# Batch 0's attention in its own order, and its global values from the common gather

## The chip, the cores and the metric

The kernel runs on one core of one Trainium2 chip. The metric is device time in microseconds (us) of one execution; several executions are timed and their median is given. The profile is one further execution, taken by the hardware profiler. Engines are named as in the profile: PE is TensorE, DVE is VectorE, ACT is ScalarE, POOL is GpSimd and SP is SyncE; PEq, DVEq and so on are their sequencers.

## The reference

Two layers are computed one after the other. The first is attention with a local window and eight global tokens, over 8 batches, 8 heads, 576 tokens and a head size of 64:

```
scores = q @ k.T / sqrt(64)
mask   = |i - j| <= 32, or i is global, or j is global
attn   = softmax(scores where mask, else -1e9)
x      = attn @ v                      # (4608 tokens, 512)
```

The second takes x through two matrix products with a periodic activation between them:

```
h   = x @ w_in                         # 512 -> 2048
g   = h + sin(alpha*h)**2 / (alpha + 1e-9)
out = g @ w_out                        # 2048 -> 512, f32
```

## The kernel before, in words

The kernel goes through the batches in order. `phase_a(b, b - 1)` computes the attention of batch b and fills TensorE's spare time with the second matrix product (`gemm2`, handed out in small steps by `fill`) of the batch before; `gemm1(b)` then computes the first matrix product and the activation of batch b in 16 groups of 128 hidden columns. All instructions are issued in an order written out by hand: each engine takes its own in program order, so an instruction that waits holds up all behind it on its engine. DMA queues are two: POOL issues the loads that convert from f32 to bf16, SP all others, each in program order as well.

**Attention (L840 to L1000).** Heads are taken in four pairs. `scores(hp, g)` (L862) computes one half of a pair's scores into a PSUM tile of two banks, ACT takes the exponential (L881), and DVE multiplies by the 0/1 mask (L882). `denominators` (L938) multiplies the exponentials by ones; ACT takes the logarithm (L830) and DVE sums the global columns (L814). `inverse` (L943) is an exponential of the negative logarithm on ACT (L837). `numerators` (L946) multiplies the exponentials by the values (L910), for batches 0 and 1 also by the global values `VGT` (L926), and DVE normalises into `xT` (L953). PSUM has the tiles `zn`, `zd` and `ring` (or, after `ring` is released, `zr`) of two banks and `zo[0]`, `zo[1]` of one. In batch 0 the first scores go to `ring`, the second scores of pairs 0 and 1 to `zn`, and those of pairs 2 and 3 to `ring`, since numerators use `zn`. The numerators of pair 0 are computed between the two scores of pair 3.

**What batch 0 does beside its scores.** `beside(at)` in `phase_a` (L1285) is called after each pair. For batch 0 it turns the keys and queries of pairs 2 and 3 with TensorE transposes from `lie[0]`, a stretch of `H2`, into `zo` (L681), and copies them to `KX` and `QX` (L688, L695). After pair 1 `first_values` (L759) builds the global values of batch 0: `g0["v"]`, an indirect DMA of batch 0's rows alone (L628), is spread and masked on DVE (L761), a product with the 0/1 matrix `pick` (L620) puts each row into its place, and DVE copies the bank to `VGT[0]` (L623). After pairs 2 and 3, half of the heads each time, DVE copies the odd value rows (`odd_rows`, L416) and the edge tiles (`edge_tiles`, L423) within the value buffer `VF[0]`, which `load_v0` fills with twelve DMAs from POOL (L396).

**The common gather.** SP gathers the rows of the eight global tokens for all batches: keys, queries, values (`gather_heads`, L538; `gather`, L544), each as eight DMAs of which one brings 64 rows of 256 bytes. A DMA of `gather_heads` writes to 64 partitions, one of `gather` to eight. POOL casts them (L772 to `gkq`, L775 to `VGb`) when batch 0's `gemm1` is under way; `turn_kq` (L777) transposes keys and queries on TensorE into `zo[1]`, DVE copies them out (L789), and POOL places batch 1's (L378, L381).

**`gemm1(0)` (L1086 to L1159).** Group nt takes one of `zn`, `zr`, `zd` in turn (L1104), ACT computes Sin (L1148), ACT or DVE squares it (L1151, L1153), DVE adds and writes `H2` (L1154). Lists name the groups that carry other work: `TURNED` transposes a pair of batch 1 into `zo`, `PLACED` copies it out, `GLOBALS` has `turn_kq`; after the last group of the batch stands the picking of batch 1's global values (L1128, with the copy on ACT).

**Others that the change touches.** `warm(z, n)` (L603) issues n products of 512 columns whose result is not used. `find_columns` (L1164) is seven small DVE instructions (L1168 to L1180) that run after the last pair of batch 3's attention.

## Time and profile before

| what | us |
|---|---|
| median of three runs | 356.49 (354.37 to 357.08) |
| the profiled execution's own time | 354.67 |
| its span, first to last instruction | 352.9 |
| batch 0's first scores begin | 11.55 |
| batch 0's first Sin (group 0 of `gemm1(0)`) | 37.38 |
| batch 0's last Sin (group 15) | 58.83 |
| batch 1's first scores begin | 60.38 |

Three views are used. The page gives the busy time of each engine over the span. The chain of waits goes back from the last instruction, at each step to what released it, and is listed in order of time: start, length, and the engine, tile and line. The timeline lists instructions in order of time, neighbours of one line merged (x2 means two): start, length, engine, line, operation, out<-in, shapes, and in brackets how long the engine had been idle and what ended that. L numbers are lines of the kernel before.

### The profile page before, as it was taken

The page shows a single profiled execution, that of the slowest core. Times are in us where ns is not written, and L with a number is a line of the kernel's source. Part 1 is how long each engine was busy: PE and PEld are TensorE (multiplying, and loading weights), DVE is VectorE, ACT ScalarE, POOL GpSimd, SP SyncE. Part 2 cuts the span into 40 slices and gives each one's busy share as a digit, 9 for nine tenths or more (in the row PEclk, how much of TensorE's full clock was granted, in tenths as well). Part 3 has the DMA queues.
Part 4 walks back from the last instruction along what each step waited for, and adds up shares of the span by engine and source line. Part 5 has one row for each costly group of instructions (what it writes and reads, how often), then busy time and mean ns, then how long its engine had stood idle before and what let it go on. Part 6 is the DMA issues. An engine that isn't in the chain of part 4 may idle for free.

```text
span 352.9 us, 11594 instructions
## 1 busy us (share of the span) xinstructions
PE 311.5 (88%) x4783; PEld 203.8 (58%) x4843; DVE 278.4 (79%) x544; ACT 282.1 (80%) x408; POOL 56.4 (16%) x89
## 2 busy tenths in 40 slices
PE   0656888889899999979999999899999999999993
PEld 0544665456655676557655675577556755665543
DVE  5977597967998788888888887978797788788940
ACT  9744789878888888978898889989898888888711
POOL 7963001230004000300003000400000000002600
PEclk9999999999999999999999999999999999999998
DMA  7999997799484948499628991792824111010232
GB/s 103 109 167 208 202 233 158 133 172 207 69 159 86 195 91 167 97 194 145 118 63 166 202 125 48 162 180 39 186 53 106 30 32 63 5 31 2 75 91 66
DMA packets 80413, 41.80 MB, mean 118 GB/s; under 512 B 65522, under 2 KB 74082, under 8 KB 79970
## 3 DMA queue, kind: packets, MB, share of 16 engines
q0 software_dynamic: 38992, 18.51, 41.3%
q1 hardware_dynamic: 41362, 22.48, 28.4%
q8 instruction: 39, 0.64, 0.7%
q14 instruction: 20, 0.16, 0.2%
HBM read 41.87 MB, written 20.77 MB: 178 GB/s over the span
## 4 chain that ended last, share of the span: by engine, by line
PE 68%; DVE 14%; ACT 7%; issue 7%; DMA 1%; POOL 1%; DVEq 0%; POOLq 0%; ACTq 0%
PE zo L1203 27%; PE zn L1104 13%; PE zr L1104 9%; PE zd L1104 9%; PE ring L872 3%; DVE H L1154 3%; ACT sb L1148 2%; PE zn L910 2%; PE zd L910 2%; DMA g0k<-in_k_dram,grow 1%; ACT E L881 1%; DVE s L1153 1%; DVE QX L363 1%; DVE E L882 1%; DVE xT L953 1%
## 5 line engine op out<-in xcount | busy, mean ns | idle before, releaser
L1203 PE MATMUL zo<-w_out,H 128*128 128x512 bf16 (+1 forms) x516 | 134.0, 376 | 6.0 <-issue 5.2
L1104 PEld LDWEIGHTS <-w_in 128*128 128x128 bf16 x1024 | 100.1, 98 | 49.9 <-issue 14.8
L1203 PEld LDWEIGHTS <-H 128*128 128x128 bf16 x592 | 53.6, 98 | 46.1 <-POOL H L1193 0.2
L1104 PE MATMUL zn<-xT,w_in 128*128 128x288 bf16 (+1 forms) x384 | 57.8, 290 | 7.2 <-DVE GN L814 3.9
L881 ACT ACTIVATE E<-ring 128x720 bf16<-128x720 f32 x48 | 37.4, 780 | 15.3 <-PE ring L872 14.5
L1104 PE MATMUL zr<-xT,w_in 128*128 128x288 bf16 x320 | 48.5, 290 | 0.2 <-DVE H L1154 0.2
L1148 ACT ACTIVATE sb<-zn,alphaT 128x576 bf16<-128x576 f32 (+1 forms) x48 | 35.6, 742 | 14.7 <-PE zn L1104 14.3
L1154 DVE SCALAR_TENSOR_TENSOR H<-s,recipT,zn 128x576 bf16<-128x576 bf16 (+1 forms) x48 | 39.5, 822 | 9.9 <-ACT s L1151 5.9
L1104 PE MATMUL zd<-xT,w_in 128*128 128x288 bf16 x320 | 46.3, 288 | 1.0 <-DVE H L1154 0.9
L1153 DVE TENSOR_TENSOR s<-sb 128x576 bf16<-128x576 bf16 (+1 forms) x70 | 32.7, 467 | 11.4 <-ACT sb L1148 11.1
L1151 ACT ACTIVATE s<-sb 128x576 bf16<-128x576 bf16 (+1 forms) x58 | 40.0, 689 | 1.8
L882 DVE TENSOR_TENSOR E<-E,MASKT 128x720 bf16<-128x720 bf16 x64 | 33.4, 529 | 9.1 <-ACT E L881 7.4
L1154 DVE SCALAR_TENSOR_TENSOR H<-s,recipT,zd 128x576 bf16<-128x576 bf16 (+1 forms) x40 | 32.9, 822 | 7.8 <-ACT s L1151 5.3
L1154 DVE SCALAR_TENSOR_TENSOR H<-s,recipT,zr 128x576 bf16<-128x576 bf16 (+1 forms) x40 | 32.9, 822 | 5.7 <-ACT s L1151 4.1
L1148 ACT ACTIVATE sb<-zd,alphaT 128x576 bf16<-128x576 f32 (+1 forms) x40 | 29.5, 738 | 5.8 <-PE zd L1104 5.8
L1148 ACT ACTIVATE sb<-zr,alphaT 128x576 bf16<-128x576 f32 (+1 forms) x40 | 29.6, 739 | 4.9 <-PE zr L1104 4.9
L1210 ACT COPY osb<-zo 128x512 f32<-128x512 f32 (+1 forms) x36 | 20.9, 582 | 11.2 <-PE zo L1203 7.5
L872 PEld LDWEIGHTS <-KX 64*64 64x64 bf16 x896 | 16.1, 112 | 20.6 <-issue 20.4
L837 ACT ACTIVATE R<-L,shift 128x576 f32<-128x576 f32 x32 | 24.9, 782 | 0.4
L348 POOL COPY seen<-xT 1x1 bf16<-1x1 bf16 x4 | 1.9, 480 | 136.4 <-DVE GN L814 136.4
L1193 POOL COPY H<-H 128x11 bf16 (+1 forms) x16 | 7.2, 452 | 98.7 <-DVE H L1154 97.9
L953 DVE TENSOR_TENSOR xT<-zn,R 128x576 bf16<-128x576 f32 x24 | 18.1, 754 | 3.0 <-PE zn L926 2.0
(179 smaller groups left out, 361.1 us busy)
## 6 DMA issues: line engine op xcount, KB each, us to landing
VF<-vd SPq DMA_DIRECT2D x24, 168.0 KB
kd<-in_k_dram POOLq DMA_DIRECT2D x6, 576.0 KB, 6.1
qd<-in_q_dram POOLq DMA_DIRECT2D x6, 576.0 KB, 11.6
vd<-in_v_dram POOLq DMA_DIRECT2D x6, 576.0 KB, 15.2
w_in<-in_moe_w_in_dram POOLq DMA_DIRECT2D x2, 1024.0 KB
w_out<-in_moe_w_out_dram POOLq DMA_DIRECT2D x2, 1024.0 KB, 22.2
out_dram<-osb SPq DMA_DIRECT2D x7, 256.0 KB
out_dram<-osb SPq DMA_DIRECT2D x8, 224.0 KB
```

The lines of the kernel that those rows point to most:

```text
L837: nc.scalar.activation(out=R[:], in_=L[:], func=AF.Exp, scale=-1.0, bias=shift[:, 0:1])
L872: nc.tensor.matmul(out=z[half * D : (half + 1) * D, t, 0 : G3 * WCOL].rearrange("p (m x c) -> p m x c", x=2, c=60)[:, m % G3, :, c0:c1], l ...
L881: nc.scalar.activation(out=Eg, in_=z[:, :, 0 : G3 * WCOL], func=AF.Exp, scale=scale)
L882: nc.vector.tensor_tensor(out=Eg, in0=Eg, in1=MASKT[:, None, G3 * g : G3 * (g + 1), :].rearrange("p o m c -> p o (m c)").to_broadcast([P, ...
L953: nc.vector.tensor_tensor(out=xT[:, hp, 0:S].rearrange("p (k m c) -> p k m c", k=4, c=KT), in0=tokens(nd(hp, 0)), in1=Rs[hp][:], op=ALU.mult,)
L1104: nc.tensor.matmul(out=h_part, lhsT=w_in[:, c, nt * P : (nt + 1) * P], rhs=xT[:, c, lo:hi], start=(c == 0), stop=(c == CT - 1), skip_group ...
L1148: nc.scalar.activation(out=sb[:, 0:W], in_=h, func=AF.Sin, scale=alphaT[:, nt : nt + 1])
L1151: nc.scalar.activation(out=s2[:, 0:W], in_=sb[:, 0:W], func=AF.Square)
L1153: nc.vector.tensor_tensor(out=s2[:, 0:W], in0=sb[:, 0:W], in1=sb[:, 0:W], op=ALU.mult)
L1154: nc.vector.scalar_tensor_tensor(out=H2[:, nt, r0 : r0 + W], in0=s2[:, 0:W], scalar=recipT[:, nt : nt + 1], in1=h, op0=ALU.mult, op1=ALU.add,)
L1203: nc.tensor.matmul(out=ops[:, cols], lhsT=H2[:, nt, blk * P : (blk + 1) * P], rhs=w_out[:, nt, cols], start=(nt == 0), stop=(nt == NT - 1) ...
L1210: nc.scalar.copy(out=osb[:, cols], in_=ops[:, cols])
```

## The change

1. Batch 0's attention has an order of its own (`first_batch`). All scores come first, alternating between `ring` and `zn`; denominators of pair hp - 1 follow the scores of pair hp. Then `ring` is released, and inverses and numerators of pairs 0 and 1 follow, the denominators of pair 3, the numerators of pair 2, those of pair 3. Numerators use `zr` (pairs 0 and 2), `zn` (pair 1) and `zd` (pair 3). Between these steps stand eleven products of `warm`; the one of before is gone.
2. Beside the scores: pairs 2 and 3 are turned after pairs 0 and 2 (keys copied on DVE, queries on ACT); after pair 1 stands only the reciprocal of alpha; after pair 3 the global values are picked and the odd rows and edge tiles of all heads are copied at once.
3. The indirect gather of batch 0's values, its spreading on DVE and the tiles for it are gone. SP's common gather of the values moves ahead of those of keys and queries, and POOL's cast of them stands between the loads of the two halves of `w_in`. `pick[:, 0]` is now masked to batch 0's rows as `pick[:, 1]` was to batch 1's.
4. In `gemm1(0)`: batch 1's global values are picked at group 1 (copy on DVE), where the cast of keys and queries stands as well; `turn_kq` moves from group 12 to 3, with batch 1's placing of globals, the loads of batch 1's values and batch 2's keys and queries behind it; the turning of batch 1's pairs moves by two groups.
5. `find_columns` moves from batch 3's attention to group 8 of `gemm1(2)`.

```diff
--- before.py
+++ after.py
@@ -581,18 +581,16 @@
         out=rowf[0 : NG * B, 4:5], in0=rowf[0 : NG * B, 0:1], scalar=float(S), in1=rowf[0 : NG * B, 3:4], op0=ALU.mult, op1=ALU.add
     )
     nc.vector.tensor_copy(out=grow[:], in_=rowf[0 : NG * B, 4:5])
-    mine = setup.tile([NG * B, B], DT.bfloat16, name="mine")
-    own = rowf[0 : NG * B]
-    nc.vector.tensor_scalar(out=mine[:], in0=jrow[0 : NG * B], scalar1=own[:, 0:1], scalar2=None, op0=ALU.is_equal)
-    one = setup.tile([NG * B, 1], DT.float32, name="one")
-    nc.vector.tensor_scalar(out=one[:], in0=own[:, 0:1], scalar1=1.0, scalar2=None, op0=ALU.is_equal)
-    nc.vector.tensor_scalar(
-        out=pick[:, 0], in0=place8[0 : NG * B], scalar1=own[:, 2:3], scalar2=None, op0=ALU.is_equal
-    )
-    nc.vector.tensor_scalar(
-        out=pick[:, 1], in0=place8[0 : NG * B], scalar1=own[:, 2:3], scalar2=one[:, 0:1], op0=ALU.is_equal,
-        op1=ALU.mult,
-    )
+    of_batch = setup.tile([NG * B, 2], DT.float32, name="of_batch")
+    for b in range(2):
+        nc.vector.tensor_scalar(
+            out=of_batch[:, b : b + 1], in0=rowf[0 : NG * B, 0:1], scalar1=float(b), scalar2=None, op0=ALU.is_equal
+        )
+    for b in range(2):
+        nc.vector.tensor_scalar(
+            out=pick[:, b], in0=place8[0 : NG * B], scalar1=rowf[0 : NG * B, 2:3], scalar2=of_batch[:, b : b + 1],
+            op0=ALU.is_equal, op1=ALU.mult,
+        )
     nc.vector.memset(KX[0][:, :, :, NK:D], 0.0)
     nc.vector.memset(VE[0][:], 0.0)
     nc.vector.memset(shift[:], -SHIFT * LN2)
@@ -622,7 +620,7 @@
     def place_picked(b, z, copy):
         copy(out=VGT[b][:].rearrange("p h d -> p (h d)"), in_=z[:])
 
-    g0 = {name: setup.tile([NG * B, D], DT.bfloat16, name="g0" + name) for name in ("k", "q", "v")}
+    g0 = {name: setup.tile([NG * B, D], DT.bfloat16, name="g0" + name) for name in ("k", "q")}
 
     def rows_of(name, src):
         nc.gpsimd.indirect_dma_start(
@@ -637,9 +635,11 @@
     for half in range(2):
         nc.gpsimd.iota(qpos[half * D : half * D + D], pattern=[[KT, NT6], [1, 2], [2, 24]], base=half * HALF,
                        channel_multiplier=0, allow_small_or_imprecise_dtypes=True)
-    rows_of("v", v)
+    gather(v, gv)
     load_v0()
-    load_w_in((0, 1))
+    load_w_in((0,))
+    nc.gpsimd.tensor_copy(out=VGb[:], in_=gv.rearrange("p h d -> p (h d)"))
+    load_w_in((1,))
     for hps in (early, late):
         for w in (1, 0):
             load_lying(1, w, hps)
@@ -648,7 +648,6 @@
     load_w_out((1,))
     gather_heads(k, gk)
     gather_heads(q, gq)
-    gather(v, gv)
 
 
     band = setup.tile([P, 2, 2, WCOL // 2], DT.bfloat16, name="band")
@@ -666,7 +665,6 @@
 
     small = tc.alloc_tile_pool(name="small", bufs=1, space=PSUM)
     both = small.tile([P, 512], DT.float32, name="pg")
-    gv0 = setup.tile([NG * B, H, D], DT.bfloat16, name="gv0")
     act, dve = nc.scalar.copy, nc.vector.tensor_copy
 
     def bank_of(z):
@@ -756,23 +754,17 @@
     place_lying(0, 0, 1, banks_of[1][0], dve)
     small.release()
 
-    def first_values():
-
-        nc.vector.tensor_tensor(
-            out=gv0[:], in0=g0["v"][:, None, :].to_broadcast([NG * B, H, D]),
-            in1=mine[:, :, None].to_broadcast([NG * B, H, D]), op=ALU.mult,
-        )
-        pick_rows(0, gv0[:].rearrange("p h d -> p (h d)"), zo[0])
-        place_picked(0, zo[0], dve)
+    def lay_global_values(b, z, copy):
+        pick_rows(b, VGb[:], z)
+        place_picked(b, z, copy)
+
+    def set_recip():
         nc.vector.tensor_scalar(out=recipT[:], in0=alphaT[:], scalar1=1e-9, scalar2=None, op0=ALU.add)
         nc.vector.reciprocal(out=recipT[:], in_=recipT[:])
 
     def cast_globals_kq():
         for w, src in ((1, gk), (0, gq)):
             nc.gpsimd.tensor_copy(out=gkq[w][:], in_=src)
-
-    def cast_globals_v():
-        nc.gpsimd.tensor_copy(out=VGb[:], in_=gv.rearrange("p h d -> p (h d)"))
 
     def turn_kq():
 
@@ -860,7 +852,7 @@
             ]
 
         def scores(hp, g):
-            z = {(0, 1): zd if b else zn, (1, 1): zn}.get((hp, g), zs)
+            z = {(0, 1): zd, (1, 1): zn}.get((hp, g), zs) if b else (zs, zn)[g]
             for e in range(NT6 + 1):
                 for half in range(2):
                     i, m, c0, c1 = windows(half)[e]
@@ -890,7 +882,10 @@
         def nd(hp, key):
 
 
-            t = (zn, zd)[key] if hp < NHP - 1 else (pair["zr"] if key else zd)
+            if b == 0:
+                t = zd if key or hp == last else (pair["zr"], zn)[hp % 2]
+            else:
+                t = (zn, zd)[key] if hp < last else (pair["zr"] if key else zd)
             return t[:].rearrange("p k (x c) -> p k x c", x=2)
 
         def products(hp, key):
@@ -956,16 +951,51 @@
             )
             global_sums(b, hp, 0, nd(hp, 0))
 
+        def release_ring():
+            ring.release()
+            pair["after"] = tc.alloc_tile_pool(name="after", bufs=1, space=PSUM)
+            pair["zr"] = pair["after"].tile([P, 2, 512], DT.float32, name="zr")
+
+        def first_batch():
+
+            for hp in range(NHP):
+                Es[hp] = pairp.tile([P, 2, NT6, WCOL], DT.bfloat16, name="E")
+                for g in range(2):
+                    scores(hp, g)
+                beside(hp)
+                if hp:
+                    denominators(hp - 1)
+            release_ring()
+            warm(zo[1], 2)
+            for hp in range(2):
+                inverse(hp)
+                numerators(hp)
+                warm(zo[1], 2)
+            denominators(last)
+            warm(zo[1], 1)
+            inverse(2)
+            numerators(2)
+            warm(zo[1], 2)
+            products(last, 0)
+            global_products(last)
+            inverse(last)
+            nc.scalar.preload_act_table(AF.Sin)
+            warm(zo[1], 2)
+            normalise(last)
+            pair["after"].release()
+
         last = NHP - 1
+        if b == 0:
+            first_batch()
+            return
         fill(START)
         beside(-1)
         for hp in range(NHP):
             Es[hp] = pairp.tile([P, 2, NT6, WCOL], DT.bfloat16, name="E")
             scores(hp, 0)
-            if hp > 1 and (b or hp == last):
-                done = hp - 2 if b else 0
-                inverse(done)
-                numerators(done)
+            if hp > 1:
+                inverse(hp - 2)
+                numerators(hp - 2)
                 fill(FIRST[hp])
             scores(hp, 1)
             if hp and 0 < b and b + 1 < B:
@@ -974,13 +1004,7 @@
                 denominators(hp - 1)
             fill(SECOND[hp])
             beside(hp)
-        if b == 0:
-            warm(zo[0], 1)
-            inverse(1)
-            numerators(1)
-        ring.release()
-        after = tc.alloc_tile_pool(name="after", bufs=1, space=PSUM)
-        pair["zr"] = after.tile([P, 2, 512], DT.float32, name="zr")
+        release_ring()
         inverse(last - 1)
         numerators(last - 1)
         denominators(last)
@@ -997,7 +1021,7 @@
         if b == B - 1:
             global_columns(slice(last, NHP))
         beside(NHP)
-        after.release()
+        pair["after"].release()
 
     def global_rows(bs):
 
@@ -1080,7 +1104,7 @@
     ON_ACT_FIRST = (1, 3, 5, 7, 9, 11, 13, 14)
     ON_ACT_SECOND = (1, 3, 5, 7, 9, 10, 12, 13)
 
-    TURNED, PLACED, GLOBALS = (4, 6, 8, 10), (5, 7, 9, 11), 12
+    TURNED, PLACED, GLOBALS = (6, 8, 10, 12), (7, 9, 11, 13), 3
     PLACED_LATE = {4: 0, 5: 1, 7: 2, 8: 3, 10: 4, 11: 5, 13: 6, 14: 7}
 
     def gemm1(b):
@@ -1115,18 +1139,17 @@
                 hp = PLACED.index(nt)
                 for w, copy in ((1, nc.vector.tensor_copy), (0, nc.scalar.copy)):
                     place_lying(1, w, hp, banks_of[NHP - 1][w], copy)
-            if b == 0 and nt == TURNED[0]:
+            if b == 0 and nt == 1:
+                lay_global_values(1, zo[0], nc.vector.tensor_copy)
                 cast_globals_kq()
+            if b == 2 and nt == NT // 2:
+                find_columns()
             if b == 0 and nt == GLOBALS + 1:
 
+                cast_qk(2)
                 load_v1()
-                cast_qk(2)
-                cast_globals_v()
                 for part in range(3):
                     place_globals(1, part, nc.gpsimd.tensor_copy)
-            if b == 0 and nt == NT - 1:
-                pick_rows(1, VGb[:], zo[0])
-                place_picked(1, zo[0], nc.scalar.copy)
             if more and nt == SOON:
                 put_globals(slice(0, SOON))
             if nt == 0:
@@ -1284,23 +1307,25 @@
     def phase_a(b_att, b_moe):
         def beside(at):
 
-            if b_att == 0 and 0 <= at < 2:
-                hp = at + 2
-                turn_lying(0, hp, banks_of[hp])
-                place_lying(0, 1, hp, banks_of[hp][1], nc.scalar.copy if at else nc.vector.tensor_copy)
-                place_lying(0, 0, hp, banks_of[hp][0], nc.vector.tensor_copy)
-            if b_att == 0 and at == 1:
-                first_values()
-            if b_att < 2 and at in ((2, 3), (0,))[b_att]:
-                hs = slice(0, H) if b_att else slice((at - 2) * H // 2, (at - 1) * H // 2)
-                odd_rows(b_att, hs, nc.vector.tensor_copy)
-                edge_tiles(b_att, hs, nc.vector.tensor_copy)
-            if b_moe is None:
+            if b_att == 0:
+                copy = nc.vector.tensor_copy
+                if at in (0, 2):
+                    hp = 2 + at // 2
+                    turn_lying(0, hp, banks_of[hp])
+                    place_lying(0, 1, hp, banks_of[hp][1], copy)
+                    place_lying(0, 0, hp, banks_of[hp][0], nc.scalar.copy)
+                if at == 1:
+                    set_recip()
+                if at == 3:
+                    lay_global_values(0, zo[0], copy)
+                    odd_rows(0, slice(0, H), copy)
+                    edge_tiles(0, slice(0, H), copy)
                 return
+            if b_att == 1 and at == 0:
+                odd_rows(1, slice(0, H), nc.vector.tensor_copy)
+                edge_tiles(1, slice(0, H), nc.vector.tensor_copy)
             if at == 2 and b_att == B - 1:
                 global_rows(slice(0, B - 1))
-            if b_att == 3 and at == 3:
-                find_columns()
             if b_att == 5 and at == 3:
                 load_columns()
             if 0 <= at < 2:
```

## The prediction

> **What bounds the kernel now.** I read the page's head first, then the chain of waits over batch 0's attention, then the timeline there, engine by engine. The sums below are made against this execution: its span, and its own time of 354.67 us, 1.8 us of which lie around the span. The three timed runs gave a median of 356.49 us (354.37 to 357.08).
>
> ```profile
> span 352.9 us, 11594 instructions
> PE 311.5 (88%) x4783; PEld 203.8 (58%) x4843; DVE 278.4 (79%) x544; ACT 282.1 (80%) x408; POOL 56.4 (16%) x89
> ...
> PEclk9999999999999999999999999999999999999998
> ```
>
> Over the whole kernel TensorE is the busiest, at 88%. The change touches mainly the first 61 us, where it is not. The chain there (start, length, what):
>
> ```profile
> 22.80 1.32 DVE VF L416
> ...
> 30.60 0.76 DVE xT L953
> ...
> 31.55 0.79 PE zn L910 x25
> ...
> 37.38 0.75 ACT sb L1148
> ```
>
> At 37.38 the first Sin of batch 0's first matrix product begins; I call this the hand-over. Before 31.55 the chain runs through VectorE: the value copies of L416 and L423 stand in its queue between the mask products, and TensorE waits for it. So the first question is when VectorE is done with these copies, the second how long TensorE needs from there.
>
> ```profile
> 12.19 0.77 ACT L881 ACTIVATE E<-ring 128x720 bf16<-128x720 f32 x1 [0.68 <-PE ring L872]
> ...
> 14.97 0.65 ACT L830 ACTIVATE L<-zd 128x576 f32<-128x576 f32 x1
> ...
> 16.44 0.64 ACT L688 COPY KX<-zo 128x576 bf16<-128x576 bf16 x1 [0.83 <-PE zo L681]
> ...
> 18.52 0.69 DVE L623 CAST VGT<-zo 128x512 bf16<-128x512 f32 x1 [0.70 <-PE zo L620]
> ...
> 21.19 0.53 DVE L882 TENSOR_TENSOR E<-E,MASKT 128x720 bf16<-128x720 bf16 x1 [0.87 <-ACT E L881]
> ...
> 22.01 2.12 DVE L416 COPY VF<-VF 24x1536 bf16<-24x1536 bf16 x2
> ...
> 22.25 1.49 POOL L402 DMA_DIRECT2D vpd<-in_v_dram  x1
> ...
> 24.16 0.93 DVE L423 COPY VE<-VF 24x256 bf16<-24x256 bf16 x4
> ...
> 27.59 1.39 DVE L416 COPY VF<-VF 24x1536 bf16<-24x1536 bf16 x2
> ...
> 29.00 1.57 DVE L423 COPY VE<-VF 24x256 bf16<-24x256 bf16 x4
> ...
> 62.91 1.94 DVE L416 COPY VF<-VF 24x3072 bf16<-24x3072 bf16 x2
> 64.88 1.19 DVE L423 COPY VE<-VF 24x512 bf16<-24x512 bf16 x4
> ```
>
> The two halves of batch 0's value copies cost 2.12 + 0.93 + 1.39 + 1.57 = 6.01 us of VectorE. Batch 1's undivided copies of the same data, with POOL quiet, took 1.94 + 1.19 = 3.13 us. Part of the difference is per-instruction cost, part lies beside POOL's work (the 1.49 us descriptor job falls on the longest copy).
>
> **The change, part by part.** *Scores without interruption.* All eight score groups run alternately in two banks, so ScalarE becomes the pacer: from 12.19, eight exponentials (6.16), now two copies of queries (1.28) and two logarithms (1.30) give 20.93. The last pair's keys are copied on VectorE behind two mask products; I add 0.55 for that (0 to 1.0). The last exponential then ends at 21.5, the last mask product 0.53 later, the copy of global values 0.69 after that: 22.7. The added reciprocal pair and the two removed small multiplications lie in VectorE's gaps.
>
> *Value copies in one piece.* 22.7 + 3.13 = 25.9, if POOL is quiet. It isn't: its weight and value loads are still being issued then. The before shows 2.9 us lost to split and collision together; I take 1.0 for collisions (0 to 2.0). VectorE is done at 26.9 (25.9 to 27.9). The last pairs' masks no longer queue behind copies.
>
> *TensorE from there.* Rows:
>
> ```profile
> 25.14 0.49 PE L926 MATMUL zn<-E,VGT 56*64 56x144 bf16 x8
> ...
> 31.55 0.76 PE L910 MATMUL zn<-E,VF 56*64 56x88 bf16 x24 [3.48 <-DVE GN L814]
> ...
> 32.34 0.84 PE L910 MATMUL zr<-E,ones 56*64 56x88 bf16 x28
> ...
> 32.95 0.79 PE L910 MATMUL zd<-E,VF 56*64 56x88 bf16 x24
> ...
> 33.97 1.62 PE L1104 MATMUL zn<-xT,w_in 128*128 128x288 bf16 x6
> ...
> 37.43 1.14 PE L1104 MATMUL zd<-xT,w_in 128*128 128x288 bf16 x8
> ...
> 66.66 1.03 PE L1203 MATMUL zo<-w_out,H 128*128 128x512 bf16 x4 [0.16 <-issue]
> ...
> 75.41 0.48 PE L910 MATMUL zn<-E,VF 56*64 56x88 bf16 x24
> ...
> 76.51 0.30 PE L926 MATMUL zd<-E,VGT 56*64 56x144 bf16 x8
> ...
> 191.19 0.90 PE L1104 MATMUL zn<-xT,w_in 128*128 128x288 bf16 x6 [0.54 <-DVE GN L814]
> ...
> 193.11 0.74 ACT L1148 ACTIVATE sb<-zn,alphaT 128x576 bf16<-128x576 f32 x1 [0.65 <-PE zn L1104]
> ```
>
> TensorE has two speeds here: six products took 1.62 us at 33.97, eight took 1.14 us at 37.43, though the granted clock (PEclk above) reads nine tenths or more in every slice; so the speeds have to be read from durations. The fast one came within about 5.3 us after dense work began at 31.55 (36.8). In the new order dense work begins when the large copies end, about 25.7, so by this row the fast speed comes at about 31.0.
>
> Slow part after 26.9: rest of the first numerators 0.50; second numerators 0.79 (31.55 to 32.34); last denominators 0.61 (32.34 to 32.95); and five filler products of 512 columns. One such costs (1.62 less a 0.2 tail) / 6 x 512/288 = 0.42. Sum 0.50 + 0.79 + 0.61 + 2.10 = 4.0, which is 30.9, just where the fast speed is due. Fast part: third and fourth numerators together 1.05 (the stretch 75.41 to 76.81 is 1.40 and holds a denominator too; shared as the slow 0.79 and 1.02 in 2.42); four fillers at (1.03 - 0.16)/4 = 0.22, 0.88; first matrix product to first Sin 1.92 (191.19 to 193.11). Sum 3.85. Hand-over 26.9 + 4.0 + 3.85 = 34.75: **2.6 us earlier**. With the copies undisturbed (1.0) and 2 us more at the fast speed (0.9) it is 4.5 earlier; with TensorE slow throughout (0.50 + 0.79 + 0.61 + 0.79 + 1.02, nine fillers 3.78, and the old 3.41 of 33.97 to 37.38, 10.9) it is 37.8, 0.4 later. The 5.3 us row is the nearest to the new stretch, and I take it.
>
> ScalarE is not late next:
>
> ```profile
> 27.20 1.44 ACT L837 ACTIVATE R<-L,shift 128x576 f32<-128x576 f32 x2
> ```
>
> The last denominators begin at 29.9 (26.9 + 0.50 + 0.84 + 0.79 + 0.84). About 0.9 later (32.34 to 33.2 in the before) comes the logarithm, 0.65, then two inverses, 1.44, then the last normalisation, 0.76 (30.60 in the chain): 33.6. The matrix product needs it for its last quarter only, at about 34.3.
>
> [...]
>
> *Values from the common gather.* Now the wait that the change adds:
>
> ```profile
> 9.00 6.39 SPq L538 DMA_DIRECT2D SQ<-in_k_dram  x8
> ...
> 22.05 6.87 SPq L544 DMA_DIRECT2D SQ<-in_v_dram  x8
> ...
> 28.68 1.33 POOL L772 CAST gkq<-SQ 64x512 bf16<-64x512 f32 x2
> ...
> 38.41 0.68 POOL L775 CAST VGb<-SQ 64x512 bf16<-64x512 f32 x1 [3.93 <-DMA LC<-L]
> ```
> ```profile
> DMA to landing us min/median/max: 2.9/3.6/4.4
> ```
>
> The value gather moves from SP's third place to its first: issued from 9.00 to 15.9. It lands 2.9 us later if it behaves as the value loads into VF that POOL issues in those same microseconds (the last row, over all twelve), and up to 9.5 later if as in the before (28.92 to 38.41). I take 3.6: 19.5. The cast (0.68) stands in POOL's queue, and behind it the second half of the first weights, batch 1's tiles, the second weights. These are covered by the first half of the first weights, which is issued ahead of the cast and still moving; without it they would land as much later as the cast waits. TensorE's picking product and VectorE's copy follow, needed at 22.0 minus 0.6 minus 0.68: values may land until 20.7 for nothing. Cost zero, bounds 0 and 4.7 (landing at 25.4).
>
> *Keys and queries gathered later.* Queries now end issuing at 28.9; before, they had landed by 28.68, at most 6.8 after their last issue (21.9), so 35.7, cast by 37.0. The turning product (now at group 3) is due after the product that started at 39.60, less 2.6, plus 1.1: 38.1. Nothing lost, or up to 1.0 if they take 9.5. Batch 2's key and query loads are issued behind that cast on POOL, some 4 us later than now; they queue behind loads that are still moving then and are first used in batch 1's loop, so they cost nothing.
>
> *Group loop of batch 0.*
>
> ```profile
> 39.60 0.65 PE L1104 MATMUL zn<-xT,w_in 128*128 128x288 bf16 x4 [1.03 <-DVE H L1154]
> ...
> 55.67 1.08 DVE L1153 TENSOR_TENSOR s<-sb 128x576 bf16<-128x576 bf16 x1
> ...
> 57.65 1.14 PE L1104 MATMUL zn<-xT,w_in 128*128 128x288 bf16 x8 [0.93 <-DVE H L1154]
> ...
> 154.24 0.90 PE L1104 MATMUL zn<-xT,w_in 128*128 128x288 bf16 x6 [1.77 <-DVE GN L814]
> ```
>
> Batch 1's picked values go from the end, where TensorE waits 0.93, into the hole of 1.03 at group 1. The wait at 57.65 comes from a square slowed to 1.08 beside POOL's placing of globals; that moves to group 4 with it, and is not saved. I take 0.5 saved (0 to 0.9).
>
> *Column finding* leaves batch 3's attention, where TensorE waited 1.77 against 0.54 in batch 4 (191.19): 1.2 gained. It enters group 8 of batch 2's loop, where VectorE's results free banks for a TensorE without holes; the same work may cost the same 1.2. I take 0 (1.2 either way).
>
> *Sum:* -2.6 - 0.5, and I give back 0.3, as batch 1's own inputs may be late when everything is earlier (its value copies at 62.91 show only that the data had landed by then). **-2.8 us: 351.9 of this execution's 354.67, or 0.79%, which makes 353.7 of the median.**
>
> **Rivals.** *A: TensorE stays slow until the matrix product.* For: the dense small products of 11.5 to 16.4 did not speed it up. Against: eleven full-size fillers, two of them ahead of 26.9. Hand-over 37.8, less 0.5: about as before, 356.4.
>
> *B: the gathered values come late (slower).* Every engine in batch 0 then hangs on one gather: TensorE's picking product stands ahead of the third denominators, VectorE's copy ahead of all value copies. Landing at 25.4, with 20.7 free, costs 4.7 against the 2.8: +1.9, 358.4. It turns into a loss from a landing at about 23.5. For: the before's 9.5 us. Against: that was beside large weight packets; the value loads at the new place land in 2.9 to 4.4.
> [...]
>
> *C: the gain is real but eaten later,* by queries that hold up the turning product (1.0) and column finding (1.2): -0.6, 355.9.
>
> *D: everything goes well,* copies undisturbed, early speed, columns free: -4.5 - 0.5 - 0.5, 351.0.
>
> **How the numbers follow.** Forecast 0.50 (353.7, its own range 352.0 to 355.2), A 0.17, B 0.11, C 0.10, D 0.12. Range 350.8 to 357.3: it holds the forecast, A, C and most of D, and leaves out half of B. About 1% (3.6 us) is what a measurement of this kernel can tell from no change. D and the upper third of the forecast are faster by more: 0.28. Only an extreme B is slower by more: 0.08. Within 1%: 0.64.
>
> **What would show it.** Right: the last exponential of batch 0 ends near 21.5; two value copies of 3072 elements follow at about 22.7; VectorE is done with them near 26.9; filler and numerators leave TensorE no hole; products of 288 columns are fast from the start of the matrix product; first Sin at 34 to 35.5; no wait at the turning product; the 1.77 of batch 3 becomes about 0.5, with a new hole in batch 2's loop. Wrong: POOL's cast of the values after 21.5, a picking product that waits, slow products at the hand-over, or a first Sin after 37.

## The result, and the profile after

The kernel after takes 353.11 us (median of 20 runs, 351.74 to 354.00); the kernel before, in 20 runs beside it, 354.75 (353.05 to 357.98). The ratio is 0.9936, 95% interval 0.9913 to 0.9960: 0.64% faster, where 0.79% was forecast. This ratio, like those below, is formed from all comparable executions and not from the medians, whose ratio is 0.9954: twelve executions of the kernel before took 353.1 to 355.1 and eight 356.1 to 358.0, so that its mean is 355.27, against 353.01 after. The profiled execution took 353.56 us, 1.11 less than that of before (354.67), with a span of 351.9. The head of its page, as that of before:

```profile
span 351.9 us, 11606 instructions
PE 314.4 (89%) x4793; PEld 203.2 (58%) x4853; DVE 275.2 (78%) x537; ACT 282.1 (80%) x408; POOL 56.0 (16%) x88
```

TensorE is busy 2.9 us longer, the fillers among it, in a shorter span; VectorE has 3.2 us less to do, 1.9 of it in the value copies (6.01 to 4.09).

Batch 0's attention on VectorE (start, length, engine, line, operation, out<-in; in brackets the idle time before and what ended it), from the timeline of the kernel after:

```profile
20.45 1.19 DVE L874 TENSOR_TENSOR E<-E,MASKT 128x720 bf16<-128x720 bf16 x2 [1.30 <-ACT E L873]
21.57 0.68 DVE L621 CAST VGT<-zo 128x512 bf16<-128x512 f32 x1
22.28 2.19 DVE L416 COPY VF<-VF 24x3072 bf16<-24x3072 bf16 x2
24.50 1.90 DVE L423 COPY VE<-VF 24x512 bf16<-24x512 bf16 x4
```

The last mask product ends at 21.6 and VectorE is done with the value copies at 26.40 (24.50 + 1.90); forecast were 22.0 and 26.9. Then TensorE and the first Sin, same view:

```profile
26.46 0.49 PE L921 MATMUL zr<-E,VGT 56*64 56x144 bf16 x8
26.89 1.04 PE L603 MATMUL zo<-ones 128*128 128x512 bf16 x2
27.85 0.76 PE L905 MATMUL zn<-E,VF 56*64 56x88 bf16 x24
...
29.81 0.79 PE L905 MATMUL zd<-E,ones 56*64 56x88 bf16 x28
30.53 0.61 PE L603 MATMUL zo<-ones 128*128 128x512 bf16 x1
31.07 0.76 PE L905 MATMUL zr<-E,VF 56*64 56x88 bf16 x24
...
32.05 0.82 PE L603 MATMUL zo<-ones 128*128 128x512 bf16 x2
32.80 0.48 PE L905 MATMUL zd<-E,VF 56*64 56x88 bf16 x24
...
33.82 0.90 PE L1128 MATMUL zn<-xT,w_in 128*128 128x288 bf16 x6
...
35.73 0.74 ACT L1171 ACTIVATE sb<-zn,alphaT 128x576 bf16<-128x576 f32 x1 [1.80 <-PE zn L1128]
```

There is no hole after 26.46, and the six products of 288 columns take 0.90 at once, as forecast. But the products of the third numerators at 31.07 are still slow (0.76), those of the fourth at 32.80 fast (0.48): the fast speed came at about 32.3, not 31.0. The first Sin begins at 35.73, 1.65 earlier than before (37.38) instead of 2.6.

The gathers: POOL's casts and the first product on their result (all gathered rows lie in one tile, `SQ`, and the bracket names the DMA whose signal was seen last, which need not be the one that the cast needs).

```profile
18.69 0.61 POOL L641 CAST VGb<-SQ 64x512 bf16<-64x512 f32 x1 [1.33 <-DMA SQ<-in_k_dram]
19.85 0.61 PE L618 MATMUL zo<-VGb,pick 64*128 64x512 bf16 x1
29.71 0.61 POOL L767 CAST gkq<-SQ 64x512 bf16<-64x512 f32 x1 [2.54 <-DMA SQ<-in_q_dram]
35.41 0.61 POOL L767 CAST gkq<-SQ 64x512 bf16<-64x512 f32 x1 [5.08 <-DMA LC<-L]
39.02 0.68 PE L776 MATMUL zo<-identb,gkq 64*64 64x32 bf16 x32
```

The values had landed by 18.7. The prediction had them free until 20.7; with VectorE's copy of `VGT` at 21.57 instead of 22.0 it is 20.3. The cast of the queries ends at 36.0 and the turning product runs at 39.02 in one piece. Neither waits.

Later, three waits of TensorE decide what is left of the gain:

```profile
115.81 0.90 PE L1128 MATMUL zr<-xT,w_in 128*128 128x288 bf16 x6 [1.05 <-DVE QX L363]
...
130.06 1.14 PE L1128 MATMUL zd<-xT,w_in 128*128 128x288 bf16 x8 [1.10 <-DVE H L1177]
...
153.23 0.90 PE L1128 MATMUL zn<-xT,w_in 128*128 128x288 bf16 x6 [0.54 <-DVE GN L806]
```

The 1.10 at 130.06 is `find_columns` in batch 2's group 8; the 0.54 at 153.23 stands where the kernel before waited 1.77. The 1.05 at 115.81 was not forecast. First and last Sin of each batch give the account (a negative number means earlier than before):

| point | before | after | difference |
|---|---|---|---|
| batch 0, first Sin | 37.38 | 35.73 | -1.65 |
| batch 0, last Sin | 58.83 | 56.59 | -2.24 |
| batch 1, last Sin | 98.82 | 96.58 | -2.24 |
| batch 2, first Sin (behind the 1.05) | 118.01 | 116.98 | -1.03 |
| batch 2, last Sin (behind the 1.10) | 136.25 | 136.45 | +0.20 |
| batch 3, first Sin (0.54 for 1.77) | 156.15 | 155.14 | -1.01 |
| end of the span | 352.88 | 351.86 | -1.02 |

### The profile page after: what moved, and what is told of

Its sections match the earlier page's. It is cut to its first block, busy times and chain, and to the rows that moved or that the text cites. A ratio compares the mean times of both kernels' runs of the same rounds, so it can differ in the third digit from the quotient of the medians.

```text
span 351.9 us, 11606 instructions
## 1 busy us (share of the span) xinstructions
PE 314.4 (89%) x4793; PEld 203.2 (58%) x4853; DVE 275.2 (78%) x537; ACT 282.1 (80%) x408; POOL 56.0 (16%) x88
## 4 chain that ended last, share of the span: by engine, by line
PE 63%; DMA 11%; DVE 9%; issue 6%; SPq 5%; ACT 4%; POOL 0%; DVEq 0%; ACTq 0%; POOLq 0%
PE zo L1226 28%; PE zn L1128 11%; PE zr L1128 9%; PE zd L1128 8%; DMA kd<-in_k_dram 6%; PE ring L864 3%; DVE H L1177 3%; DMA SQ<-in_q_dram 2%; DMA kt<-kd 2%; SPq L544 2%; DVE QX L363 2%; PE zn L905 2%; PE zd L905 2%; SPq L538 2%; ACT sb L1171 1%
## 5 line engine op out<-in xcount | busy, mean ns | idle before, releaser
L1128 PE MATMUL zn<-xT,w_in 128*128 128x288 bf16 (+1 forms) x384 | 57.0, 287 | 4.5 <-DVE GN L806 2.7
L1128 PE MATMUL zr<-xT,w_in 128*128 128x288 bf16 x320 | 47.7, 287 | 1.3 <-DVE QX L363 1.0
L873 ACT ACTIVATE E<-ring 128x720 bf16<-128x720 f32 x46 | 36.0, 782 | 10.5 <-PE ring L864 9.9
L1176 DVE TENSOR_TENSOR s<-sb 128x576 bf16<-128x576 bf16 (+1 forms) x70 | 32.3, 462 | 11.7 <-ACT sb L1171 11.4
L822 ACT ACTIVATE L<-zd 128x576 f32<-128x576 f32 x25 | 16.7, 669 | 8.1 <-PE zd L905 7.9
```

Of the source, the lines that this page charges most:

```text
L822: nc.scalar.activation(out=L[:], in_=den, func=AF.Ln, scale=2.0**-SHIFT)
L873: nc.scalar.activation(out=Eg, in_=z[:, :, 0 : G3 * WCOL], func=AF.Exp, scale=scale)
L1128: nc.tensor.matmul(out=h_part, lhsT=w_in[:, c, nt * P : (nt + 1) * P], rhs=xT[:, c, lo:hi], start=(c == 0), stop=(c == CT - 1), skip_group ...
L1176: nc.vector.tensor_tensor(out=s2[:, 0:W], in0=sb[:, 0:W], in1=sb[:, 0:W], op=ALU.mult)
```

## The experiments

Each is the kernel after with an edit, unless it says otherwise. The kernel before was run beside them (medians 354.2 to 355.9 by group), so ratios are to compare, and for single steps the times of the profiles, of which there is one for each kernel. "Hand-over" is batch 0's first Sin.

**Column finding.** Back to batch 3's attention:

```
-            if b == 2 and nt == NT // 2:
-                find_columns()
+            if b_att == 3 and at == 3:
+                find_columns()
```

> The kernel after with find_columns back in batch 3's attention, nothing else changed. Theory (its 1.2 us are paid wherever VectorE is needed at once): TensorE's hole of 1.1 us in group 8 of batch 2's matrix product is gone, the wait of 1.77 us at the start of batch 3's matrix product (0.54 in the kernel after) is back, and the time is that of the kernel after within 0.3 us: 353.1, ratio to before 0.993 to 0.997. Rival (the move was worth its forecast gain of 1.2 and the hole at group 8 is made good later): 1.2 us slower than the kernel after, ratio 0.998.

352.82 us, ratio 0.994 (0.9915 to 0.9965). Where TensorE waited in batch 3:

```profile
151.88 0.90 PE L1128 MATMUL zn<-xT,w_in 128*128 128x288 bf16 x6 [1.78 <-DVE GN L806]
```

The 1.78 is back, and batch 2's loop has no hole: from batch 2's first exponential to batch 3's first Sin it is 56.43 us (97.36 to 153.79), with the columns at group 8 56.51 (98.63 to 155.14). The move is worth nothing, as forecast. Into batch 0's attention, behind the reciprocal after pair 1:

```
                 if at == 1:
                     set_recip()
+                    find_columns()
```

> The kernel after with find_columns in batch 0's attention, behind the reciprocal after pair 1, where VectorE has idle time between mask products. Theory (only its place costs): both holes are gone, the one of 1.1 us in batch 2's group 8 and the 1.77 in batch 3, nothing is paid in batch 0 (last exponential still at 21.1 plus or minus 0.2): 1.0 to 1.2 us faster than the kernel after, ratio to before about 0.990. Rival (seven small VectorE instructions hold up the next mask products and the key copies of the last pair): last exponential and hand-over up to 1.2 later, time as the kernel after.

352.18 us, ratio 0.9922 (0.9892 to 0.9952). Between the same two points it is now 55.19 us (98.98 to 154.17), 1.3 less: both holes are gone. In batch 0 it is not quite free; the hand-over is at 36.10, 0.37 later than in the kernel after. The rest of the gain stays.

**Fillers and TensorE's speed.** No fillers at all (the eleven products of the six `warm` calls in `first_batch` are left out; the result does not use them):

> The kernel after without its eleven filler products. Theory 1 (TensorE speeds up about 5 to 6 us after its last hole, whatever products fill the time; the attention products alone are dense enough from 26.4): fast products still from about 32, first Sin at 33.3 to 34.5 instead of 35.7, 1 to 2 us faster than the kernel after. Theory 2 (the full-size fillers are what brings the fast speed): first Sin at about 34.5, but the products of 288 columns are slow (1.6 us for six) at the start of the matrix product and for some 2 to 4 us after it, and batch 0's last Sin comes as late as in the kernel after (56.6) or up to 1.5 later.

350.54 us, ratio 0.9899 (0.9866 to 0.9931).

```profile
26.03 0.49 PE L921 MATMUL zr<-E,VGT 56*64 56x144 bf16 x8
26.27 0.80 PE L905 MATMUL zn<-E,VF 56*64 56x88 bf16 x24
...
29.94 1.49 PE L1123 MATMUL zn<-xT,w_in 128*128 128x288 bf16 x6
31.26 0.90 PE L1123 MATMUL zr<-xT,w_in 128*128 128x288 bf16 x6
...
32.44 0.74 ACT L1166 ACTIVATE sb<-zn,alphaT 128x576 bf16<-128x576 f32 x1 [1.17 <-PE zn L1123]
```

The first six products are slow (1.49), the next six fast: the speed comes at about 31.1 without a single filler, and the hand-over is 3.29 earlier than in the kernel after, more than theory 1 asked. The fillers behind VectorE's copies only stood in the way. How much they cost depends on the execution: the four profiled kernels that have all eleven (the kernel after, the two with the columns moved, and the one with its own gather further down) hand over at 35.73, 34.36, 36.10 and 35.33, which is 9.3, 8.2, 9.3 and 8.5 after VectorE's end. Without fillers it is 6.5, so against this one execution their price is 1.8 to 2.9; the other 0.4 of the 3.29 is VectorE's end, 25.97 here and 26.40 in the kernel after. Ten instead of two ahead of the first numerators, the others kept:

```
-            warm(zo[1], 2)
+            warm(zo[1], 10)
```

> The kernel after with ten instead of two filler products ahead of the first numerators: they fill the stretch 22 to 26 in which TensorE waits three times for the value copies. Theory (the step that was mis-sized is the beginning of dense work, 26.4 and not 25.7, because the holes of 1.15, 0.96 and 0.56 us still count): without the holes dense work begins at 21, the fast speed comes at 26.5, the nine later fillers and the numerators cost half, first Sin at 32.5 to 33.5 instead of 35.7, time 2 to 3 us less than the kernel after, ratio to before about 0.986. Rival (holes of one microsecond don't matter, fast speed still comes at about 32.4): the fillers only push the first numerators back, first Sin at 36 to 36.5.

351.61 us, ratio 0.9896 (0.9856 to 0.9937).

```profile
21.14 3.60 PE L603 MATMUL zo<-ones 128*128 128x512 bf16 x10
24.66 0.48 PE L905 MATMUL zr<-E,VF 56*64 56x88 bf16 x24
25.86 0.20 PE L905 MATMUL zr<-E,VE 56*64 56x32 bf16 x2 [0.71 <-DVE VE L423]
```

Ten products in 3.60 us, where ten slow ones would take about 4.4 by the prediction's 0.42 each and its tail of 0.2: the speed came among them, and the hole of 0.71 did not take it away (0.20 for the two products behind it, 0.23 in the kernel after). Hand-over 33.18. Of this 2.55 only 1.0 is left at the end of the span (350.84 against 351.86): 1.4 goes into a wait of 1.34 at the turning product, since the queries were cast only at 37.57, and a wait of 1.72 that the profile puts down to nothing (issue) follows in batch 1. The best place is the hole alone (eight, none behind):

```
             release_ring()
-            warm(zo[1], 2)
+            warm(zo[1], 8)
... (the five later calls are left out)
```

> The kernel after with eight fillers ahead of the first numerators, in TensorE's hole of 2.1 us and beyond it, and none behind. Theory (what speeds TensorE up is the dense time before the copies end, what slows the kernel are the nine fillers behind them): TensorE is fast from about 24, six products of the matrix product take 0.9 from its start instead of 1.49, first Sin 0.6 to 1.2 earlier than without any filler (31.2 to 31.8); what of it lasts depends on batch 1's values, which landed at 58.2: time as without fillers within 0.5. Rival (the tail without fillers is set by ScalarE's logarithm, two inverses and the last normalisation, not by TensorE's speed): first Sin within 0.4 us of 32.4.

350.57 us, ratio 0.9899 (0.9855 to 0.9942). Hand-over 30.99, earlier than expected, but batch 0's loop takes 23.85 us instead of the 20.86 without fillers, and the time is that without fillers.

```profile
36.21 0.61 PE L776 MATMUL zo<-identb,gkq 64*64 64x32 bf16 x16 [1.50 <-POOL gkq L767]
36.75 2.10 PE L1124 MATMUL zr<-xT,w_in 128*128 128x288 bf16 x8
```

Half of the 3.0 is the wait of 1.50 at the turning product. The other half is speed: behind it the products are slow again, eight in 2.10 us instead of 1.15. The profile's granted clock, 1.00 elsewhere in this stage, is 0.50 from 35.9 to 39.3. Why this wait cost the speed is open, since 1.34 in the kernel with ten fillers did not. Two pairs fewer, those behind the first and second numerators:

```
                 numerators(hp)
-                warm(zo[1], 2)
```

> The kernel after without the two pairs of fillers behind the first and second numerators (four products fewer). Theory on the fillers: each costs the path its own duration, 0.42 slow, so first Sin 1.4 to 1.8 us earlier than 35.7, at about 34.1; the fast speed comes at the same time, 31 to 32.5. Theory on the wait of 1.05 us in batch 2 (it goes with the number of TensorE instructions ahead of it: 1.0 in all kernels with the same number as the kernel after, 0.7 with three fewer, none with eleven fewer): about 0.5. Rival on the wait (chance of the run): 0 or 1.0.

One run, 350.99 us beside 354.21. Hand-over 33.98, 1.75 earlier: the expected price of four slow fillers, though the kernels with all fillers differ among themselves by as much. The wait in batch 2 is 0.44, where 0.5 was expected:

```profile
113.93 0.40 PE L1127 MATMUL zr<-xT,w_in 128*128 128x288 bf16 x2 [0.44 <-issue]
```

Last, the kernel before with eight fillers in its hole of 3.48 us, and nothing else:

```
             inverse(1)
             numerators(1)
+            warm(zo[0], 8)
```

> The kernel before, unchanged but for eight fillers behind the second numerators, where its TensorE waited 3.48 us for VectorE's value copies. Theory (a good half of what the new order brought could be had by this alone, because the kernel before began its matrix product at the slow speed): six products take 0.9 instead of 1.62 from the start of the matrix product, first Sin at 34.8 to 35.6 instead of 37.38, time 1.8 to 2.5 us less than before, ratio 0.993 to 0.995. Rival (fillers in a hole bring nothing because the next step is bound by VectorE and ScalarE): first Sin at 36.8 to 37.4, ratio 0.998 to 1.000.

353.14 us, ratio 0.9948 (0.9913 to 0.9983).

```profile
28.00 3.20 PE L605 MATMUL zo<-ones 128*128 128x512 bf16 x8
31.60 0.48 PE L910 MATMUL zn<-E,VF 56*64 56x88 bf16 x24 [0.41 <-DVE GN L814]
...
33.31 0.90 PE L1105 MATMUL zn<-xT,w_in 128*128 128x288 bf16 x6 [0.31 <-DVE GN L814]
...
35.39 0.74 ACT L1149 ACTIVATE sb<-zn,alphaT 128x576 bf16<-128x576 f32 x1
```

The numerators that took 0.76 there take 0.48, the six products 0.90 instead of 1.62. With the old order, the hand-over is at 35.39, about where the kernels with the new order and all its fillers have it (34.36 to 36.10).

**Source of the values.** Batch 0's global values from an indirect gather of their own, as before:

```
+    rows_of("v", v)
     load_v0()
...
-                    lay_global_values(0, zo[0], copy)
+                    own_values()
```

> The kernel after, but batch 0's global values come again from an indirect gather of their own, spread and masked on VectorE after pair 1 as before; the common gather keeps its new order. Theory (the order of the work is the whole gain, the source of the values gives nothing as long as they land in time): the last exponential, the value copies and the hand-over within 0.4 us of the kernel after (21.1, 26.4, 35.7), time within 0.5 us of it. Rival (the common gather is part of the gain): POOL's indirect gather pushes every value load back by 1.0 us and VectorE's spreading (0.67) holds up masks and the last pair's keys: hand-over 0.7 to 1.7 later than in the kernel after.

352.86 us, ratio 0.9932 (0.9904 to 0.9959); hand-over 35.33. The common gather gives no time of its own. VectorE's copies show what the 1.0 us of collisions depends on, since against the kernel after they start 0.35 later here and POOL's issue of batch 1's values 0.64 earlier (23.07 to 24.80):

```profile
22.63 2.96 DVE L416 COPY VF<-VF 24x3072 bf16<-24x3072 bf16 x2
25.61 1.19 DVE L423 COPY VE<-VF 24x512 bf16<-24x512 bf16 x4
```

Both large issues (second weights, batch 1's values) fall on the first two copies: 1.02 more than the 1.94 of batch 1's there, nothing on the others.

**Batch 1's values and POOL's issues.** In the kernel without fillers a new wait appeared, in VectorE's rows:

```profile
58.27 2.02 DVE L416 COPY VF<-VF 24x3072 bf16<-24x3072 bf16 x2 [0.94 <-DMA VF<-vpd]
```

No fillers, and the load of these values sooner:

```
+    cast_v1()
     load_w_out((0,))
-    cast_v1()
```

> The kernel after without fillers, and POOL issues the load of batch 1's values ahead of the first half of the second weights instead of behind it. Theory (in the kernel without fillers batch 1's value copies waited 0.94 us for their data, which is where 1.0 of the 3.3 us gained at the hand-over went): the data land 1 to 4 us sooner than 58.2, the wait is gone, batch 2's first scores come 1.0 earlier than in the kernel without fillers, time 0.7 to 1.0 us less than it (ratio to before 0.987). Rival (the load is limited by the whole queue of loads, not by its place in it): the wait stays between 0.6 and 1.2, time as the kernel without fillers.

351.22 us, ratio 0.9883 (0.9827 to 0.9939). The wait is gone; from batch 1's first exponential to batch 2's it is 39.99 us instead of 40.98. But the span is 348.7, no shorter than the 348.4 without it: batch 0's loop takes 22.13 instead of 20.86, as the queries were cast at 36.14 and the turning product waited 0.80. The same, with the second weights issued behind the edge tiles:

```
                     edge_tiles(0, slice(0, H), copy)
+                    pace(VE[0][96:97, 0, 0:1])
+                    load_w_out((0,))
+                    load_w_out((1,))
```

> As the kernel with batch 1's values sooner (no fillers), but POOL issues both loads of the second weights only when VectorE has finished the edge tiles. Theory (the 1.0 us by which batch 0's value copies, 2.19 + 1.90, are longer than batch 1's 1.94 + 1.19 comes from POOL writing descriptors at the same time): the edge tiles take 1.2 to 1.3 instead of 1.90, VectorE is done 0.6 to 1.0 earlier and so is the hand-over (about 31.6 against 32.4). Rival (the copies are slow for another reason, such as partitions or transfers that land then): same durations within 0.2, same hand-over.

351.33 us, ratio 0.9886 (0.9839 to 0.9934), span of the profile 347.3.

```profile
22.27 2.64 DVE L416 COPY VF<-VF 24x3072 bf16<-24x3072 bf16 x2
24.94 1.20 DVE L423 COPY VE<-VF 24x512 bf16<-24x512 bf16 x4
```

The edge tiles take 1.20 as expected, but now the issue of batch 1's values (1.87 from 22.26) falls on the value copies, 2.64 instead of 2.19; 3.84 in all against 4.09, so 0.25 is saved and not 0.6 to 1.0. So the collision is real and moves with POOL's issue. The time is that with the values sooner alone (351.22); the profiled execution is the fastest of eight. The hand-over is at 31.93, mostly because the matrix product was fast from its start here (six products 0.91).

**All of it together.** Eight fillers in the hole, none behind; batch 1's value load ahead of its key and query loads; the second weights behind the edge tiles; `GLOBALS` 5 instead of 3; `find_columns` in batch 0:

```
+    cast_v1()
     for hps in (early, late):
         for w in (1, 0):
             load_lying(1, w, hps)
-    load_w_out((0,))
-    cast_v1()
-    load_w_out((1,))
...
-    TURNED, PLACED, GLOBALS = (6, 8, 10, 12), (7, 9, 11, 13), 3
+    TURNED, PLACED, GLOBALS = (6, 8, 10, 12), (7, 9, 11, 13), 5
```

> The kernel after with what the experiments point to: eight fillers in TensorE's hole ahead of the first numerators and none behind; batch 1's value load issued ahead of batch 1's key and query loads, the second weights behind the edge tiles; the turning of the gathered keys and queries at group 5 instead of 3; find_columns in batch 0. Theory (these are separate costs, each on the path once those before it are gone): first Sin at 30.3 to 31.0, the group loop without a wait at the turning product (batch 0's last Sin 20.9 later), no wait for batch 1's values, no hole in batch 2's group 8: span 346 to 347, time 347.8 to 349, ratio to before 0.978 to 0.983. Rival (another input of batch 1 is late next, such as its turned keys or the second weights): batch 1's first Sin no earlier than 74.2, time 350 to 351 as without fillers.

347.55 us (346.67 to 349.73), ratio 0.9789 (0.9749 to 0.9828), span 345.4.

```profile
22.26 1.51 POOL L482 DMA_DIRECT2D H<-in_k_dram  x1
22.72 1.93 DVE L416 COPY VF<-VF 24x3072 bf16<-24x3072 bf16 x2
22.83 1.93 POOL L482 DMA_DIRECT2D H<-in_q_dram  x1
24.69 1.19 DVE L423 COPY VE<-VF 24x512 bf16<-24x512 bf16 x4
...
30.77 0.74 ACT L1163 ACTIVATE sb<-zn,alphaT 128x576 bf16<-128x576 f32 x1 [0.41 <-PE zn L1122]
```

The copies are as short as batch 1's in the kernel before (1.94 and 1.19), the hand-over is at 30.77, batch 0's last Sin at 52.09, 4.5 earlier than in the kernel after, and all of it arrives at the end of the span (345.38 against 351.86; the rest of the 6.5 is 1.2 for the columns and the wait of batch 2, 0.40 here instead of 1.05). The DMA engines moved as much during the copies as in the kernel after (207 GB/s, and 205 to 209 there), so it is not the amount of transfers that lengthens VectorE's copies there. Its counterpart with `GLOBALS` at 3:

> The combined kernel, but with the turning product at group 3 as in the kernel after. Theory (the gathered queries land at 35 to 37.5 whatever the attention does, so that an earlier hand-over runs into them): TensorE waits 1.0 to 2.0 us for POOL's cast at the turning product, and batch 0's last Sin comes 1.0 to 2.0 us later than in the combined kernel. Rival (the wait seen without later fillers came from the weights that moved with them, not from the gather's own place): no wait above 0.3, same time.

348.49 us, ratio 0.9795 (0.9749 to 0.9841).

```profile
34.06 0.42 PE L774 MATMUL zo<-identb,gkq 64*64 64x32 bf16 x16
35.06 0.61 POOL L765 CAST gkq<-SQ 64x512 bf16<-64x512 f32 x1 [4.82 <-DMA SQ<-in_q_dram]
35.72 0.42 PE L774 MATMUL zo<-identb,gkq 64*64 64x32 bf16 x16 [1.24 <-POOL gkq L765]
```

TensorE waits 1.24 in the middle of the turning product, and batch 0's last Sin is 1.20 later (53.29). Over the kernels with the new order this cast began between 34.98 (combined) and 37.57 (ten fillers), at 35.41 in the kernel after, however early the hand-over was.

## Why the prediction was right, point by point

The forecast, 0.79% faster, lies in the measured interval (0.40% to 0.87%). Its terms were not all right, and in part the number is luck: the sum was made against the profiled execution, for which it gave 2.8 us, and there the change brought 1.1. The means differ by 2.26; what makes up the rest no trace shows.

**Scores, right.** Last mask product 21.6 (forecast 22.0); ScalarE paces them, but for waits of 0.42 and 0.77, the second for scores that wait for the last pair's keys. The sum came out so well because it was also too long elsewhere: it counted an exponential at its 0.77, and in a row one starts every 0.66.

**Value copies, right in place and size.** 2.19 + 1.90 = 4.09 where 3.13 + 1.0 was forecast. That the 1.0 is POOL's doing was argued then and is shown now: the copies are 1.93 + 1.19 with POOL's large issues elsewhere, and the surplus follows the issues from one group of copies to the other. The surplus is not the length of the issue: beside the 1.41 of the second weights (22.31 to 23.72) the first copy took 0.95, as batch 1's with POOL quiet in the before, the second 1.21 (23.26 to 24.47), and the edge tiles beside the 1.67 of batch 1's values (23.71 to 25.38) 1.90 for 1.19. In the combined kernel the small key and query issues beside the copies get longer instead (1.51 and 1.93 for 0.58 each in the kernel after). By what means one engine lengthens the other's work no run shows.

**TensorE from there, mis-sized: the step that cost the 1 us.** From VectorE's end the forecast gave 7.85 us, it took 9.33 (26.40 to 35.73). "In the new order dense work begins when the large copies end, about 25.7, so by this row the fast speed comes at about 31.0" is the sentence that failed: the products were slow until about 32.3, so the third numerators and the fillers behind them took 1.73 (31.07 to 32.80) instead of about 1.0; and each change between fillers and numerators cost about 0.1 more than the sum of slow products had it (4.67 to 31.07, forecast 4.0). VectorE's end, 0.5 earlier than forecast, made up a third of it, and the first Sin at 35.73 lies just outside the 34 to 35.5 that were named. Two readings were off without consequence: the idle 0.16 stands ahead of the four products and was no part of their 1.03, though 0.22 a fast filler is what two took here (0.44 from 33.38 to 33.82), and the last slice of the granted clock reads 8, not 9. The point is not a property of the kernel: the one with only the columns moved back has the same TensorE instructions up to there, VectorE done at 26.13, and became fast at about 29.7, with the hand-over at 34.36:

```profile
27.58 0.76 PE L905 MATMUL zn<-E,VF 56*64 56x88 bf16 x24
...
29.53 0.54 PE L905 MATMUL zd<-E,ones 56*64 56x88 bf16 x28
...
30.33 0.48 PE L905 MATMUL zr<-E,VF 56*64 56x88 bf16 x24
```

Counted from the end of VectorE's copies, the speed came after 3.5 us here, 5.9 in the kernel after, 5.1 without fillers (26.0 to 31.1): the forecast's 5.3 was one draw. So the prediction should have given the hand-over a spread, not one value. What decides when the speed comes no run shows.

**What the prediction did not see:** fillers are priced on the path and not in the hole. It counted 2.10 + 0.88 for nine fillers as a given of the change. Without them the hand-over is at 32.44, and with them in the hole instead at 30.99. With eight of them the old order reaches 35.39. So in these executions the new order by itself is worth 37.38 - 32.44 = 4.9 us at the hand-over, and of that its own fillers give back 2.9 here, 1.8 to 2.9 over the four kernels that have them.

**Gathers, right.** Values landed by 18.7 (forecast 19.5), cost 0. The value gather had landed at most 2.8 us after its last issue ended (15.90 to 18.69), where the before left room for 9.5; the keys 7.1 (22.62 to 29.71) and the queries 5.5 (29.96 to 35.41). The queries cost 0 as well, with little to spare: the cast ended 3.0 before the turning product, and every kernel with a hand-over at 33.2 or earlier and the product at group 3 waited there, but for the one without fillers. That is the part of rival C that came true, for those.

**Group loop, right:** 0.59 gained (forecast 0.5).

**Columns, right:** 1.2 gained in batch 3, 1.2 lost in batch 2 (column experiments).

**Give-back of 0.3, wrong in size:** batch 1's inputs cost the kernel after nothing (-2.24 at batch 0's last Sin, -2.24 at batch 1's). The wait exists, from a hand-over about 2.4 earlier on (0.94 without fillers, at -3.29).

**The 1.05 at 115.81 is open.** The instruction named, a copy of `QX`, is not what the product needs: the program has it wait for VectorE's `GD`, which was done at 113.94. The wait goes with the number of TensorE instructions, as was expected of the kernel with four fewer: 0.98 to 1.05 in the kernel after and the three with as many, 0.63 with two fewer (the kernel before with eight fillers), 0.40 to 0.68 with three fewer (eight fillers in the hole, the combined kernel and its counterpart), 0.44 with four fewer, none with ten or eleven fewer (the kernel before, those without fillers). With eight more it is not there, and a wait of 1.72 stands in batch 1. Why the number should matter is open. Whether this wait is missing in other executions of the kernel after no run shows.

Rivals: A (slow throughout) did not happen. B (values late) did not: 1.6 us to spare (18.7 and 20.3). D's copies and speed were had by the combined kernel, by other edits; that this change's own edits bring the 2 us more at the fast speed that D counts on, no run shows: where the forecast had it at 31.0, it came at about 29.7 with the columns moved back and at about 32.3 here.

## What to carry to other kernels

Filler products belong where TensorE waits anyway, ahead of the work that is to be fast; behind the wait nine of them cost 1.8 to 2.9 us here, and eight of them in the old kernel's hole brought about as much as this change (ratio 0.9948, and 0.9936). In the new order what fillers in the hole alone gained was lost again at the turning product; it lasted in the combined kernel, where the load order and the group of the turning product changed as well. Before a stage is pulled forward, list what must have landed for the next one (here queries at 35 to 37.6, batch 1's values at 58): the gain ends at the first that has not, and the loads' order on their queue has to move with the stage. Where a large copy on VectorE sets the end, look at what GpSimd issues in those same microseconds (4.09 us for the copies beside two large issues here, 3.12 without them).

## What was not expected of the hardware

TensorE became fast 3.5 us after VectorE's end in one execution and 5.9 in another with the same TensorE instructions up to there, which, with VectorE's end 0.27 earlier, moved the hand-over by 1.37 us (34.36 and 35.73). It kept the fast speed over holes of 0.71 and 0.41 us, and over a wait of 1.34 with ten fillers, but lost it for 3.4 us at a wait of 1.50 with eight in the hole (granted clock 0.50 from 35.9 to 39.3). A DMA issue of 1.4 to 1.9 us on GpSimd lengthened the group of VectorE's copies beside it by 0.25 to 0.7 us, two of them together by 1.0, whichever group they lay beside; yet the first copy of the kernel after, beside an issue for nearly all its length, took 0.95, as without one.
